# Four blocks of 32 columns in place of two of 64 for the last transform stage's products

## The chip, the cores and the metric

The kernel runs on one core of one Trainium2 chip. A core has a matrix engine (TensorE, PE in the profile; its loads of stationary operands are listed apart as PEld), a vector engine (VectorE, DVE), a scalar engine (ScalarE, ACT), GpSimd (POOL) and a queue engine (SyncE, SP) that issues transfers here. The metric is the device time of one execution in microseconds, as the median of several runs.

TensorE multiplies a stationary operand, which is loaded into an array of 128 rows by 128 columns, with a moving operand. A product may take only a part of the array: the rows are those of the contraction, the columns those of the output's partitions. The profile writes the part as rows*columns: 128*64 is a stationary operand of 128 rows in 64 columns.

## The reference

Two stages follow each other. The first is a long convolution in each of 128 channels, done with Fourier transforms; the second a feed-forward layer on its result.

```python
# x, v: (4, 12544, 128); pos_emb: (12544, 64)
h_filt = (np.maximum(pos_emb @ w1, 0.0) @ w2) * np.exp(-0.01 * pos)[:, None]
u = x * v
y = irfft(rfft(u, n=2 * S, axis=1) * rfft(h_filt, n=2 * S, axis=0), n=2 * S, axis=1)[:, :S]
attn = x * y
t = attn.reshape(4 * 12544, 128)
h = np.maximum(np.maximum(t @ moe_w1, t @ moe_w2), t @ moe_w3)   # 768 wide
out = h @ moe_w_out
```

All is 32-bit floating point.

## The kernel before

The transforms are products with tables. Positions are split in two: 12544 = 98 x 128. A forward transform has a first stage over the 98 (`u_products`), a twiddled second stage over the 128, the product with the filter's spectrum, and an inverse second stage; `g_quarter` does the second stages of two groups in one call, on blocks of 64 rows by 64 columns. Its results go to DRAM (`zd`), with 90 frequencies along one axis. The last transform stage is the inverse over these 90 frequencies. It is done tile by tile, where a tile is four of the 128 positions of a batch with all 98 of the other axis, 392 tokens, so there are 32 tiles in each of 4 batches, 128 in all.

For each tile these steps follow each other:

- `t_load` (line 705) brings `zt`, two halves of 90 x 512, and every second time `x`.
- `t_sums` (line 731) makes their sum and difference on VectorE or GpSimd.
- `t_last` (line 747) does the last stage's products on TensorE. For each of four positions `s` and two tables `a` it multiplies a stationary operand of 90 rows and 128 columns, taken from `zt`, with a table `f4p` of 49 moving columns. Each result goes to its own 49 columns of one PSUM bank. VectorE then multiplies the bank with `x` into `g`, the feed-forward layer's input.
- `up` and `down` (lines 766 and 777) do the feed-forward layer with 392 moving columns: for each of six blocks `f` two products of 128 rows and the maximum, and then a product into `ops`. In the last batch `products` (line 823) does the output products in another form.

Every one of these products goes through `halves_mm` (line 152) or is written in the same way by hand: one call becomes two, one on columns 0 to 63 and one on columns 64 to 127. The two write partitions 0 to 63 and 64 to 127 of the same bank:

```python
for h in range(2):
    nc.tensor.matmul(out[64 * h:64 * h + 64], lhsT[:, 64 * h:64 * h + 64], rhs,
                     start=start, stop=stop, skip_group_check=True)
```

The order of the work is fixed by the program's text, without a scheduler. While batch `b` goes through the feed-forward layer, the convolution of batch `b + 1` runs beside it: `conv_steps` (line 609) makes a list of its steps with a slot for each, six slots to a tile, and the main loop (line 1189) runs the steps of a slot behind that slot's `up` and `down`. `t_last` for the next tile is called in slot 2, 3 or 4 of the present one (`plan[i][2]`), so a tile's products are made some slots before its own `up` needs them. In the last batch (line 1266) there is no convolution beside it, and `t_last` is called twice for each pair of tiles. In the trace the products of `t_last` stand under line 156 with the outputs `cps`, `last` and, for the first tile, `hps`.

Of the kernel before, what the change touches and what calls it, by code (L numbers as in the profile page):

```python
# [91 lines left out]
def kernel(  # L92
# [15 lines left out]
    nc = tc.nc  # L108
    NG, _, _, B, NB = x.shape
    FO, S = posT.shape  # L110
    D = w2.shape[1]
# [40 lines left out]
    def halves_mm(out, lhsT, rhs, start, stop):  # L152
# [5 lines that stand above are left out]
# [543 lines left out]
    NT = P // 4  # L701
# [45 lines left out]
    def t_last(i, bank=None):  # L747
        zt = zts.pop(i)
        ps = bank or state["bank"]()
        own = i[0] == B - 1 and i[1] > 1  # L750
        g = (lp if own else hp).tile([D, 4, NB], FP32, tag="g", name="gt", bufs=4 if own else 3)
        y = ps[:, 0:N].rearrange("d (p n) -> d p n", p=4)

        h = NB // 2
        for s in range(4):
            for a in range(2):
                halves_mm(y[:, s, a * h:a * h + h], zt[a][:, s * D:(s + 1) * D],
                          f4p[:, i[0] > 0 and i[1] >= NT // 2, a, :], s == 0 and a == 0, True)
        y = y.rearrange("d p (a m) -> d p m a", a=2)
        xT = xTs.pop(i)  # L760
        nc.vector.tensor_tensor(out=g[:].rearrange("d p (m a) -> d p m a", a=2), in0=y,
                                in1=xT.rearrange("d p (m a) -> d p m a", a=2),
                                op=ALU.mult)
        gs[i] = g

    def up(i, f, tag="hid", bufs=3):
        rhs = gs[i][:].rearrange("d p n -> d (p n)")
        h = (hidp if tag == "hid" else lp).tile([P, N], FP32, tag=tag, name="hid", bufs=bufs)
        pa = next(hbanks)
        halves_mm(pa[:, 0:N], w_sb[1][:, f * P:(f + 1) * P], rhs, True, True)  # L770
        nc.scalar.activation(h[:], pa[:, 0:N], Relu)  # L771
        pb = next(hbanks)
        halves_mm(pb[:, 0:N], w_sb[2][:, f * P:(f + 1) * P], rhs, True, True)
        nc.vector.tensor_tensor(out=h[:], in0=h[:], in1=pb[:, 0:N], op=ALU.max)  # L774
        return h
# [386 lines left out]
    f4p = hp.tile([N1, 2, 2, NB // 2], FP32, name="f4p", bufs=1)  # L1162
# [26 lines left out]
    for n, (b, i) in enumerate(tiles[:LAST]):  # L1189
        if i == 0:  # L1190
            plan, pairs_from = plans[b]
        if n == 0:
            t_load(*tiles[0], (nc.sync, nc.gpsimd))
            t_load(*tiles[1])
            second_ = []
            for h, tag in enumerate(("eo", "cb")):
                top, both = u_products(2, 2 * h, 2, next(hbanks), tag)
                top()
                second_.append(both)
            spare = state["bank"]()  # L1200
            third = u_products(3)
            fourth = u_products(4, 0, 2, spare, "xs")
            t_sums(tiles[0], nc.vector)
            for fn in second_:
                fn()
            fourth[0]()
            t_last(tiles[0], next(hbanks))
            rest = u_products(4, 2, 2, ops.tile([D, 512], FP32, tag="ops", name="ps1"), "cb")
            rest[0]()
            fourth[1]()  # L1210
        for f in range(NF):

            if i < NT - 2:
                if f == 0:
                    t_load(*tiles[n + 2])
            elif i == NT - 1 and f < 2 and n + 1 + f < len(tiles):
                t_load(*tiles[n + 1 + f])
            turn_ = i == NT - 1
            if f == 4 and n + 1 == LAST:
                t_sums(tiles[n + 2], nc.vector)  # L1220
            h = up((b, i), f)
            if n == f == 0:
                rest[1]()
            if n == 0 and f in (1, 2):
                third((f - 1,))
            for a in range(2):
                if f == plan[i][a]:
                    t_sums(tiles[n + 1],
                           nc.vector if turn_ or i * NF > pairs_from else nc.gpsimd, (a,))
            late.append(((b, i), f, h))  # L1230
            if len(late) > 2:
                down(*late.pop(0))
            if f == plan[i][2]:
                t_last(tiles[n + 1])
            if f == 5 and n + 1 == LAST:
                t_last(tiles[n + 2])
            run(besides.pop(n * NF + f, ()))
# [28 lines left out]
    for i in range(0, NT, 2):  # L1266
        h = {}
# [69 lines left out]
```

## Time and profile before

| | |
|---|---|
| median of 3 runs | 2269.55 us (2269.53 to 2269.72) |
| span of the profiled execution | 2267.5 us |
| the median lies above that span by | 2.05 us |
| PE busy | 2252.4 us, 99% |
| PEld busy | 1356.9 us, 60% |
| DVE, ACT, POOL busy | 69%, 52%, 39% |
| granted TensorE clock | 1.00 of full speed between 300 us and the end |
| DMA share, 300 to 1850 us / 1850 to 2267 us | 0.90 / 0.22 |

The span is that of one profiled execution; its rows are sums and means over that execution. The time around it (start and end of the program) is not profiled; the difference to the median is taken for it. A row of the profile's groups gives the line, the engine, the operation, what is written and read, the part of the array, the shape of the moving operand, the number of records, and then busy time, mean duration of one in ns and idle time before it. In the timeline a row is a run of like instructions: start in us, duration in us, and the number of records. A matmul's duration reaches from its start to its modelled end, and successive matmuls overlap, so the pace is read from the starts and not from the durations.

The first 284 us are the prologue (filter, first batch's transform). From about 300 to 1847 us the feed-forward layer of three batches runs with the next batch's convolution beside it; the rest is the last batch alone.

### The profile page before, as it was taken

To read this page: it belongs to the slowest core of one execution; us is meant where nothing else is said; L and a number is where in the kernel's file an instruction comes from. 1 tells how busy PE (TensorE), PEld (TensorE's weight loads), DVE (VectorE), ACT (ScalarE), POOL (GpSimd) and SP (SyncE) were. 2 spreads that over 40 slices of the span, in tenths; PEclk is the share of its full clock that TensorE was granted. 3 is DMA by queue.
4 is the path that set the end of the run, shared out by engine and by line. 5 is a ranking of instruction groups with operands and counts; after the bars stand their busy time and mean duration, and the time that the engine had idled before them with its cause. 6 is when DMAs were issued, how large, how long until landed. Compare 5 with 4: busy or idle time off the path is not lost.

```text
span 2267.5 us, 68405 instructions
## 1 busy us (share of the span) xinstructions
PE 2252.4 (99%) x27855; PEld 1356.9 (60%) x27855; DVE 1563.7 (69%) x2859; ACT 1176.0 (52%) x2131; POOL 876.7 (39%) x1090
## 2 busy tenths in 40 slices
PE   9999999999999999999999999999999999999998
PEld 8999866555555556655555556655555556666665
DVE  5589967678778667668888757667888754454443
ACT  3688844466666534456666534456666522222222
POOL 1145434223333234323333234323333326666666
PEclk9999999999999999999999999999999999999999
DMA  8788999889989599989999699889999732222221
GB/s 194 179 248 277 298 201 183 168 201 233 243 220 248 158 187 185 174 190 239 241 236 238 181 180 185 160 195 239 232 245 232 194 82 56 58 70 67 56 56 23
DMA packets 473324, 411.03 MB, mean 181 GB/s; under 512 B 327997, under 2 KB 374526, under 8 KB 473009
## 3 DMA queue, kind: packets, MB, share of 16 engines
q1 hardware_dynamic: 445929, 329.31, 64.4%
q0 software_dynamic: 26288, 75.62, 10.9%
q8 instruction: 219, 3.59, 0.7%
q10 hardware_dynamic: 792, 1.72, 0.3%
q14 instruction: 96, 0.79, 0.1%
HBM read 262.84 MB, written 84.67 MB: 153 GB/s over the span
## 4 chain that ended last, share of the span: by engine, by line
PE 99%; DMA 0%; issue 0%; ACT 0%; POOL 0%; DVE 0%; POOLq 0%; ACTq 0%; DVEq 0%
PE hps L156 45%; PE ops L156 20%; PE ops L834 6%; PE cps L428 5%; PE ps L156 4%; PE cps L156 4%; PE cps L496 3%; PE ps L165 3%; PE cps L506 3%; PE sps L1066 2%; PE gps L1048 2%; PE last L156 1%; PE ps L380 1%; PE ps L342 1%; DMA wt<-wt_const 0%; DMA zt<-zd 0%
## 5 line engine op out<-in xcount | busy, mean ns | idle before, releaser
L156 PE MATMUL hps<-gt,w_sb 128*64 128x392 f32 x6144 | 1146.2, 494 | 0.1
L771 ACT ACTIVATE hid<-hps 128x392 f32<-128x392 f32 x768 | 384.1, 500 | 699.6 <-PE hps L156 680.6
L156 PEld LDWEIGHTS hps<-gt,w_sb 128*64 128x64 f32 x6144 | 421.2, 137 | 430.8 <-issue 401.3
L774 DVE TENSOR_TENSOR hid<-hid,hps 128x392 f32<-128x392 f32 x768 | 428.0, 557 | 335.6 <-PE hps L156 323.0
L156 PE MATMUL ops<-hid,wo_sb 128*64 128x392 f32 x2304 | 477.1, 492 | 0.0
L548 POOL TENSOR_TENSOR cb<-cb,xs 128x512 f32<-128x512 f32 x135 | 173.9, 1288 | 474.7 <-DVE xs L545 384.1
L156 PEld LDWEIGHTS ops<-hid,wo_sb 128*64 128x64 f32 x2304 | 166.0, 137 | 213.1 <-issue 213.1
L521 DVE TENSOR_TENSOR cb<-cps,eo 128x512 f32<-128x512 f32 (+1 forms) x288 | 175.1, 649 | 76.1 <-ACT eo L518 76.1
L445 DVE TENSOR_TENSOR spec<-cps,high 128x360 f32<-128x360 f32 (+1 forms) x186 | 139.2, 789 | 104.7 <-ACT high L440 104.7
L789 POOL DMA_DIRECT2D out_dram<-ot x96 | 75.6, 788 | 335.2 <-ACT ot L787 282.3
L536 ACT ACTIVATE xs<-cb 32x512 f32<-32x512 f32 x270 | 169.6, 628 | 21.1 <-DVE cb L521 12.1
L537 ACT COPY xs<-cb 32x512 f32<-32x512 f32 x270 | 166.3, 616 | 3.2
L440 ACT COPY high<-cps 128x360 f32<-128x360 f32 x93 | 73.9, 797 | 169.7 <-PE cps L428 144.9
L552 DVE TENSOR_TENSOR xs<-cb 128x256 f32<-128x256 f32 x270 | 144.4, 580 | 7.7 <-POOL cb L548 7.7
L428 PEld LDWEIGHTS cps<-f1q,uT 98*64 98x64 f32 x2960 | 125.4, 137 | 26.2 <-issue 24.3
L428 PE MATMUL cps<-f1q,uT 98*64 98x90 f32 x2960 | 130.9, 241 | 0.0
L396 POOL COPY planes<-ut 128x784 uint16<-128x784 uint16 x90 | 76.3, 847 | 119.8 <-DVE ut L375 114.1
L529 POOL DMA_DIRECT2D zd<-cb x135 | 92.4, 685 | 63.7 <-DVE cb L521 60.7
L156 PEld LDWEIGHTS cps<-f4p,even 90*64 90x64 f32 x1552 | 87.5, 138 | 35.9 <-issue 34.6
L858 POOL DMA_DIRECT2D out_dram<-o x128 | 77.5, 610 | 51.5 <-DVE o L851 49.1
L156 PE MATMUL cps<-f4p,zt 90*64 90x49 f32 x1552 | 95.8, 222 | 0.0
L156 PE MATMUL cps<-f4p,even 90*64 90x49 f32 x1552 | 94.5, 220 | 0.0
(152 smaller groups left out, 3150.5 us busy)
## 6 DMA issues: line engine op xcount, KB each, us to landing
ht<-hd SPq DMA_DIRECT2D x264, 256.0 KB, 6.5
wt<-wq_const SPq DMA_DIRECT2D x144, 256.0 KB, 6.2
zd<-cb POOLq DMA_DIRECT2D x135, 256.0 KB, 5.7
zt<-zd SPq DMA_DIRECT2D x384, 90.0 KB, 3.0
sq<-spec SPq DMA_DIRECT2D x264, 128.0 KB, 6.4
ut<-in_xr_dram SPq DMA_DIRECT2D x128, 196.0 KB, 4.0
ut<-in_vr_dram SPq DMA_DIRECT2D x128, 196.0 KB, 4.4
xT<-in_x_dram SPq DMA_DIRECT2D x256, 98.0 KB, 3.4
```

Of the source, the lines that this page charges most:

```text
L156: nc.tensor.matmul(out[64 * h:64 * h + 64], lhsT[:, 64 * h:64 * h + 64], rhs, start=start, stop=stop, skip_group_check=True)
L428: nc.tensor.matmul(ps[64 * c:64 * c + 64, 256 * i + h * N1:256 * i + (h + 1) * N1], t[:, 2 * ((at + i) % 8) + h].rearrange("n r t -> n (r ...
L445: nc.vector.tensor_tensor(out=spec[:, :, a, at:at + n], in0=v[:, 1], in1=highs[0], op=op)
L521: nc.vector.tensor_tensor(out=cb[:, a, lo:hi], in0=ps[:, lo:hi], in1=eo[:, lo:hi], op=op)
L529: nc.gpsimd.dma_start(zd[b][2 * z:2 * z + 2].rearrange("k c t a f -> (k c t) a f"), zss.pop(z))
L536: nc.scalar.mul(xs[at:at + 32], xt[at + 32:at + 64], -1.0)
L537: nc.scalar.copy(xs[at + 32:at + 64], xt[at:at + 32])
L548: nc.gpsimd.tensor_tensor(out=xts[g], in0=xts[g], in1=xs[:], op=ALU.add)
L552: nc.vector.tensor_tensor(out=ab[:, q], in0=y[:, 0], in1=y[:, 1], op=(ALU.subtract, ALU.add)[q])
L771: nc.scalar.activation(h[:], pa[:, 0:N], Relu)
L774: nc.vector.tensor_tensor(out=h[:], in0=h[:], in1=pb[:, 0:N], op=ALU.max)
L834: nc.tensor.matmul(ps[64 * c:64 * c + 64, 0:H2], w, rhs[:, H2 * c:H2 * c + H2], start=start, stop=True, skip_group_check=True)
```

## The change

The inner call of `t_last` on two halves of the columns is replaced by four calls on 32 columns each. Each writes 32 partitions of the same bank. The operands, the moving table, the order over positions and tables, and the sums in PSUM are the same; only `start`'s place in the call differs, since it is set for each of the four blocks at the first position and table as it was for each of the two.

```diff
         for s in range(4):
             for a in range(2):
-                halves_mm(y[:, s, a * h:a * h + h], zt[a][:, s * D:(s + 1) * D],
-                          f4p[:, i[0] > 0 and i[1] >= NT // 2, a, :], s == 0 and a == 0, True)
+                for q in range(4):
+                    nc.tensor.matmul(y[32 * q:32 * q + 32, s, a * h:a * h + h],
+                                     zt[a][:, s * D + 32 * q:s * D + 32 * q + 32],
+                                     f4p[:, i[0] > 0 and i[1] >= NT // 2, a, :],
+                                     start=s == 0 and a == 0, stop=True, skip_group_check=True)
```

Nothing else of the kernel changes.

## The prediction

> **What bounds the kernel now.** I read the page's busy shares first, then the chain, then the timeline of TensorE around one `t_last`, and last the timeline around other work that already uses the array in another division.
>
> ```profile
> PE   2252.4 (99%) x27855; PEld 1356.9 (60%) x27855; DVE 1563.7 (69%) x2859; ACT 1176.0 (52%) x2131; POOL 876.7 (39%) x1090
> ...
> PE 99%; DMA 0%; issue 0%; ACT 0%; POOL 0%; DVE 0%; POOLq 0%; ACTq 0%; DVEq 0%
> ...
> L156 PE MATMUL cps<-f4p,zt 90*64 90x49 f32 x1552 | 95.8, 222 | 0.0
> L156 PE MATMUL cps<-f4p,even 90*64 90x49 f32 x1552 | 94.5, 220 | 0.0
> ```
>
> TensorE is busy for 99% of the span, it is 99% of the chain that ended last, and the two rows of the changed products had no idle time before them. No other engine and no DMA sets the pace here, so whatever a `t_last` gains or loses on TensorE reaches the end one for one. The question is only how long one `t_last` holds the array. Each call appears as two records: 2 x 1552 here, 2 x 480 in the last batch and 32 at the start are 4096 records for 128 tiles x 16 calls.
>
> The timeline of one `t_last` (start, us, engine, line, operation, records):
>
> ```profile
> 995.87 0.27 PE L156 MATMUL cps<-f4p,even 90*64 90x49 f32 x4
> 995.97 0.29 PE L156 MATMUL cps<-f4p,zt 90*64 90x49 f32 x4
> ...
> 996.67 0.29 PE L156 MATMUL cps<-f4p,zt 90*64 90x49 f32 x4
> 996.79 1.50 PE L156 MATMUL hps<-gt,w_sb 128*64 128x392 f32 x8
> 998.12 0.83 PE L156 MATMUL ops<-hid,wo_sb 128*64 128x392 f32 x4
> 998.78 1.49 PE L156 MATMUL hps<-gt,w_sb 128*64 128x392 f32 x8
> ```
>
> From 995.87 to 996.79 it holds the array 0.92 us. The steps of four records are 0.117 us apart in the middle (995.97 to 996.67 are six steps), so a pair of records, one on each half of the columns, takes 58.4 ns. The `hps` group behind it takes 1.33 us to its successor where four pairs of 329 ns make 1.315, so the cost is 0.935 us, 16 pairs of 58.4 ns.
>
> The timeline around one `g_quarter` (64 rows by 64 columns, four blocks at once), entered from products on 128 rows by 64 columns and left to them again. The second fence is a narrower window on its entry:
>
> ```profile
> 1000.75 1.49 PE L156 MATMUL hps<-gt,w_sb 128*64 128x392 f32 x8
> 1002.07 0.83 PE L156 MATMUL ops<-hid,wo_sb 128*64 128x392 f32 x4
> 1002.83 0.67 PE L496 MATMUL cps<-sq,wt 64*64 64x128 f32 x16
> 1003.32 0.62 PE L506 MATMUL cps<-xs,wt 64*64 64x128 f32 x16
> 1003.75 0.62 PE L496 MATMUL cps<-sq,wt 64*64 64x128 f32 x16
> 1004.19 0.62 PE L506 MATMUL cps<-xs,wt 64*64 64x128 f32 x16
> 1004.74 1.54 PE L156 MATMUL hps<-gt,w_sb 128*64 128x392 f32 x8
> 1006.10 0.50 PE L156 MATMUL ops<-hid,wo_sb 128*64 128x392 f32 x2
> ```
> ```profile
> 1002.83 0.34 PE L496 MATMUL cps<-sq,wt 64*64 64x128 f32 x4
> ```
>
> The reader is to see two things. Four blocks do run at once: four records of 0.32 us or less began within 0.02 us, and sixteen take 0.435 us (1003.32 to 1004.19 is 0.87 for 32), 109 ns for a group of four. And the division costs something at its edges: 1002.07 to 1006.10 is 4.03 us, of which 2 pairs (0.657), 16 groups (1.745) and 4 pairs (1.315) explain 3.72. The other 0.31 us stand at the borders: 0.10 before the first record (the last pair's 329 ns from 1002.40 end at 1002.73), 0.05 more in the first group (0.49 to the next line in place of 0.435), 0.11 before `hps`, 0.05 in its first group.
>
> **The change, part by part.**
>
> *Instructions.* Each `t_last` issues 32 calls in place of 16, so 64 matmul and 64 load records in place of 32 and 32: 4096 more of each over the run. Order, operands, accumulation and all other engines' work are unchanged; VectorE's multiply still waits for the last call. No DMA or wait is added or moved.
>
> *How long a group takes.* A group becomes four blocks of 32 columns. What a matmul of 49 moving columns needs on its block follows from two rows: 329 ns at 392 columns and 109 at 128 give 0.833 ns a column, so 109 - 79 x 0.833 = 43 ns at 49. That is below the 58.4 seen today, so today's pair is held by something else, and the nearest row says by what: the weight load.
>
> ```profile
> 18.36 0.44 PEld L327 LDWEIGHTS ps<-back,winT 128*105 128x105 f32 x4
> 18.36 0.58 PE L327 MATMUL ps<-back,winT 128*105 128x64 f32 x4
> ```
>
> Four loads of 105 columns took 0.44 us in all, and one lasts 0.17, so they follow at (0.44 - 0.17) / 3 = 90 ns, while 64 moving columns would need 56. With 58.4 at 64 columns, a load costs (90 - 58.4) / 41 = 0.77 ns a column, and 32 columns come to 58.4 - 25 = 34 ns. So the load falls below the matmul, and a group is held by its 43 ns. This asks that loads of four column blocks overlap as those of two do today. I take 43; the bounds are 58.4 (loads share one path by columns, nothing gained) and, far above, 104 (four records at 26 ns, below). Stream: 16 x 43.3 = 693 ns in place of 935, a gain of 242 ns for each tile.
>
> *The borders.* Today's `t_last` has the division of its neighbours (all columns in halves, 90 and 128 rows), and I see no gap there. Blocks of 32 columns are a new division, entered and left 128 times; neighbours are always `up`, `down` or `u_products`, all in halves. Is it the rows or the columns that cost? The prologue has a change of columns alone:
>
> ```profile
> 61.81 1.72 PE L165 MATMUL ps<-f1q,uT 98*64 98x90 f32 x40
> 63.46 1.08 PE L380 MATMUL ps<-eye,ut 128*98 128x128 f32 x8
> 64.47 2.24 PE L165 MATMUL ps<-f1q,uT 98*64 98x90 f32 x52
> ```
>
> Twenty pairs of 77 ns (0.833 x 90 + 2.5) from 61.81 end at 63.36, and the transposes start at 63.46: 0.10. Eight of them at 109 ns are 0.87, but `f1q` starts 1.01 after: 0.14. So a change of columns costs 0.24 before the slower first group behind it, 0.29 with it. I take 0.31, the row with four blocks; the bounds are 0 (a change within column blocks is free) and 0.32.
>
> The Trainium skill, page "TensorEngine Tiling (Array Packing)", section "Key Properties", says that a change of tiling mode drains the array; it gives no price, and this trace does: about 0.1 us at each border. The same page's "Theoretical Speedup" table promises up to 4x for 32 columns; by that rule alone a `t_last` would fall from 0.935 to 0.47 us and the kernel to about 2210 us. The rows speak for the drain and for 43 ns a group.
>
> *Sum.* 693 + 310 = 1003 ns against 935: 68 ns more for each tile, x 128 = 8.7 us. The span goes from 2267.5 to 2276.2; the runs' median of 2269.55 lies 2.05 above the span, so 2278.3 us. I hold no cover against it: TensorE has no idle time at these places to swallow it, and what runs beside it only gets more slack.
>
> **The rivals.**
>
> 1. *No drain between column blocks* (faster). If halves and quarters count as one division, only the stream's gain is left: 242 x 128 = 31 us, 2238.6 us. For it: both leave the rows whole. Against: the prologue's change of columns alone costs 0.24. It decides below 0.24 us for the two borders.
> 2. *Loads or issue hold the group.* If loads of the four blocks share their path, a group stays at 58.4 and the borders are pure loss: 310 x 128 = 40 us, 2309. For it: four loads with the same rows appear nowhere here. Against: two halves' loads overlap today, or a pair would need twice one load. An intermediate 50 ns gives +22 us.
> 3. *No four at once, or a floor for each record.* The tightest row of small products, 64 moving columns on four blocks, goes at 30 ns a record and less (line below; 26 in blocks of 64 records). At 26 ns, 64 records take 1664 ns: (1664 + 310 - 935) x 128 = 133 us, 2403. With two blocks at a time: 16 x 87 + 310 - 935, 98 us, 2368. For it: that row. Against: its loads last 197 ns where others last 133, so they may be the brake, and `g_quarter`'s four records began within 0.02 us.
>
> ```profile
> 20.63 3.02 PE ps L342 x100
> ```
>
> The page "TensorE: Matmul & The Clock Gate", section "Wait — 56ns, not 53.3ns?", puts a floor of about 25 ns between the starts of small matmuls. By that rule the sum would be near rival 3's; the starts within 0.02 us of four blocks speak against it across blocks.
>
> **How the numbers follow.** The main case (drain of 0.29 to 0.32, groups of 43 to 47 ns) has 0.62 and gives +48 to +137 ns a tile, 2275.7 to 2287 us; its centre is the forecast, 2278.3. Rival 2 in all its degrees has 0.13 (2287 to 2310), rival 3 has 0.07. Rival 1 in full has 0.08, and borders of half the price or so 0.10 (from 2253 to 2274), of which about half falls within 0.2% of before. A 0.2% change is 4.5 us, about what a measurement of this kernel can tell from none. So faster 0.13, same 0.06, slower 0.81. The range from 2268 to 2310 takes in the main case, rival 2 and the upper part of the cheap borders; outside are rivals 1 and 3.
>
> **What would show it.** In the profile after, the rows read 90*32 with 6208, 1920 and 64 records; between `t_last`'s first record and `hps` about 0.78 to 0.80 us (15 groups of 43, the last stream, then the gap of 0.1), 0.1 us of gap before the first record, and `hps` and its like behind it with a slower first group. Groups of 58 ns would show rival 2, records 20 ns or more apart rival 3, no gap rival 1. It would be wrong if TensorE waited anywhere for what comes out of `t_last`, or if the division were changed at a different price for 32-column blocks than for 64 and 98.

## The result and the profile after

The changed kernel takes 2284.02 us (2282.83 to 2288.86 in four runs) against 2269.64 before: a ratio of 1.0066, 95% interval 1.0052 to 1.0081. It is 14.4 us slower. Its four runs spread over 6 us where the four before spread over 0.4; but in the comparisons below, 13 and 21 runs of the kernel before spread over 4 and 5 us, so this spread is no sign of the change. The forecast was 2278.3 (8.7 us slower), the range 2268 to 2310. The profiled execution has a span of 2282.8 us and a time of 2284.58; the span before was 2267.5, so 15.3 us are to be found.

The page of the changed kernel, its lines on busy shares, the instruction queue, the chain and the new loads; the last line is that of the same loads before:

```profile
PE 2262.9 (99%) x31951; PEld 1328.0 (58%) x31951; DVE 1564.3 (69%) x2859; ACT 1176.1 (52%) x2131; POOL 877.0 (38%) x1090
...
q8 instruction: 251, 4.11, 0.8%
...
PE 98%; DMA 1%; issue 0%; SPq 0%; DVE 0%; POOL 0%; ACT 0%; POOLq 0%; ACTq 0%; DVEq 0%
...
L758 PEld LDWEIGHTS cps<-f4p,even 90*32 90x32 f32 x3104 | 65.0, 108 | 59.3 <-issue 49.5
...
L156 PEld LDWEIGHTS cps<-f4p,even 90*64 90x64 f32 x1552 | 87.5, 138 | 35.9 <-issue 34.6 <-DVE zt L740 0.6 <-DVE xs L545 0.4
```

TensorE issues 4096 more records of each kind, as said, and a load lasts 108 ns where it lasted 138. It is busy for only 10.5 us more, though; 4.8 us of the 15.3 are time in which it is idle (span less busy, 15.1 us before and 19.9 after). The queue of instructions brings 251 packets in place of 219.

The timeline of two `t_last` in the changed kernel:

```profile
1852.57 1.49 PE L156 MATMUL hps<-gt,w_sb 128*64 128x392 f32 x8
1853.89 0.83 PE L156 MATMUL ops<-hid,wo_sb 128*64 128x392 f32 x4
1854.65 0.29 PE L758 MATMUL cps<-f4p,even 90*32 90x49 f32 x8
1854.76 0.27 PE L758 MATMUL cps<-f4p,zt 90*32 90x49 f32 x8
...
1855.28 0.27 PE L758 MATMUL cps<-f4p,zt 90*32 90x49 f32 x8
1855.48 1.54 PE L156 MATMUL hps<-gt,w_sb 128*64 128x392 f32 x8
1856.85 0.83 PE L156 MATMUL ops<-hid,wo_sb 128*64 128x392 f32 x4
1857.61 0.29 PE L758 MATMUL cps<-f4p,even 90*32 90x49 f32 x8
```

Eight records, two groups of four blocks, follow at 0.087 us (1854.76 to 1855.28 is six steps): 43.7 ns a group. All four blocks work at once. The borders are there too: the last `ops` pair from 1854.22 would end at 1854.55, the first record stands at 1854.65; 1855.28 plus 0.087 is 1855.37 and `hps` starts at 1855.48; and `hps` needs 1.37 to its successor in place of 1.315.

Laid tile against tile, the two traces drift apart by 54 to 55 ns with nearly every `t_last`, from the first batch to the last: 128 x 0.0545 = 7.0 us. Some 8.0 us of the rest come in eight single steps, all in the first three batches, the largest of 4.2 us at the 81st tile; at five of the eight TensorE is idle for 0.34 to 2.09 us, which the profile puts to "issue". One more step, of 1.0 us, belongs to neither part: at 312 us TensorE waited 0.87 us for VectorE (`hid`), at a place which the changed kernel reached 0.6 us earlier than the kernel before. 7.0 + 8.0 + 1.0 - 0.6 is 15.4, the 15.3 but for rounding. At the 81st tile the trace shows this:

```profile
1580.57 0.29 PE L758 MATMUL cps<-f4p,even 90*32 90x49 f32 x8
...
1581.40 1.54 PE L156 MATMUL hps<-gt,w_sb 128*64 128x392 f32 x8
1582.77 0.83 PE L156 MATMUL ops<-hid,wo_sb 128*64 128x392 f32 x4
1583.53 0.67 PE L496 MATMUL cps<-sq,wt 64*64 64x128 f32 x16
1584.02 0.62 PE L506 MATMUL cps<-xs,wt 64*64 64x128 f32 x16
1584.45 0.62 PE L496 MATMUL cps<-sq,wt 64*64 64x128 f32 x16
1584.89 0.60 PE L506 MATMUL cps<-xs,wt 64*64 64x128 f32 x12
1587.58 0.44 PE L506 MATMUL cps<-xs,wt 64*64 64x128 f32 x4 [2.09 <-issue]
1587.94 2.87 PE L156 MATMUL hps<-gt,w_sb 128*64 128x392 f32 x8
1590.60 1.23 PE L156 MATMUL ops<-hid,wo_sb 128*64 128x392 f32 x4
```

TensorE stops in the middle of a run of like products that wait for nothing; the profile can only say "issue". Counted in the trace, a packet of the instruction queue started at 1585.12 and landed at 1586.25, and the products went on 1.33 us after that. Some 272 records, loads and matmuls, stand within the 4.9 us ahead of the gap, 128 of them in `t_last` and 120 in `g_quarter`. Then `hps` takes 2.66 us to its successor in place of 1.33. The table by windows shows why (window, its length, busy times, granted clock, DMA share, GB/s):

```profile
1585.00:1589.00 4.00, 1.91 (x24) 0.98 (x18) 1.03 (x2) 0.00 (x0) 1.25 (x1) 0.87 0.87 299
1589.00:1592.00 3.00, 3.00 (x14) 1.11 (x12) 1.07 (x2) 0.97 (x2) 0.00 (x0) 0.60 1.04 199
1592.00:1595.00 3.00, 3.00 (x22) 1.33 (x20) 1.30 (x4) 2.40 (x5) 0.68 (x1) 1.00 1.07 216
```

The granted clock falls behind the gap: 0.13 x 4 + 0.40 x 3 = 1.7 us of it are lost, 3.4 us at half speed, so a gap of 2.1 us costs about 4.

### The profile page after: what moved, and what is told of

It is laid out like the page before. It is cut to its first block, busy times and chain, and to the rows that moved or that the text cites. A ratio compares the mean times of both kernels' runs of the same rounds, so it can differ in the third digit from the quotient of the medians.

```text
span 2282.8 us, 76597 instructions
## 1 busy us (share of the span) xinstructions
PE 2262.9 (99%) x31951; PEld 1328.0 (58%) x31951; DVE 1564.3 (69%) x2859; ACT 1176.1 (52%) x2131; POOL 877.0 (38%) x1090
## 3 DMA queue, kind: packets, MB, share of 16 engines
q8 instruction: 251, 4.11, 0.8%
## 4 chain that ended last, share of the span: by engine, by line
PE 98%; DMA 1%; issue 0%; SPq 0%; DVE 0%; POOL 0%; ACT 0%; POOLq 0%; ACTq 0%; DVEq 0%
PE hps L156 45%; PE ops L156 19%; PE ops L837 6%; PE cps L428 5%; PE ps L156 4%; PE cps L758 4%; PE cps L496 3%; PE ps L165 3%; PE cps L506 3%; PE sps L1069 2%; PE gps L1051 2%; PE last L758 1%; PE ps L380 1%; PE ps L342 1%; DMA ut<-in_vr_dram 0%
## 5 line engine op out<-in xcount | busy, mean ns | idle before, releaser
L758 PEld LDWEIGHTS cps<-f4p,even 90*32 90x32 f32 x3104 | 65.0, 108 | 59.3 <-issue 49.5
L540 DVE TENSOR_TENSOR cb<-cb,ht 128x512 f32<-128x512 f32 x135 | 92.3, 683 | 2.5 <-ACT xs L537 2.0
L375 DVE TENSOR_TENSOR ut<-ut 128x392 f32<-128x392 f32 x128 | 78.5, 615 | 20.4 <-DMA ut<-in_vr_dram 18.9
```

The source lines that it names most:

```text
L758: nc.tensor.matmul(y[32 * q:32 * q + 32, s, a * h:a * h + h], zt[a][:, s * D + 32 * q:s * D + 32 * q + 32], f4p[:, i[0] > 0 and i[1] >= NT ...
```

## The experiments

My theory had two parts now: +54 ns a tile, from groups and borders as predicted, and gaps where TensorE runs out of instructions, because a `t_last` has twice as many and a packet comes late while transfers are dense. The rival was one cost spread over all tiles, 14.4 / 128 = 112 ns each; a second rival for the gaps was something else that comes late at those places.

### The change in the last batch alone

```diff
-                halves_mm(...)
+                if i[0] == B - 1:
+                    ...  # four blocks of 32
+                else:
+                    halves_mm(...)
```

> Four blocks of 32 columns only in the last batch's 32 tiles; the other 96 tiles keep two of 64. Theory (two parts): each tile costs +54 ns on TensorE (groups of 43.7 ns, 0.29 us at the borders), and beside it TensorE ran out of instructions in a few places while transfers are dense. The last batch has a DMA share of 0.22, so here only the first part: 32 x 0.054 = +1.7 us, 2271.3, no gaps in which TensorE waits for issue, and hardly any spread between runs. Rival (the whole +14.4 us is one cost spread over the tiles, 112 ns each): +3.6 us, 2273.2.

2271.87 us against 2270.05 (ratio 1.0007, interval 0.9997 to 1.0016): +1.8. The interval reaches from -0.7 to +3.6 us, so the times alone don't tell the theory from its rival or from no change; the trace does. In it a pair of tiles of the last batch takes 26.07 us in place of 25.96, 55 ns a tile, and no gap for issue stands in the last batch. That is the first part alone. The spread was not small, as I had expected, but 3.8 us, like that of the kernel before.

### The change in the first three batches alone

The same edit with `i[0] < B - 1`.

> Four blocks of 32 columns only in the first three batches' 96 tiles. Theory: 96 x 0.054 = 5.2 us, plus all of the gaps for issue, 7 to 8 us in the profiled run: +11 to +14 us, 2281 to 2284, with a spread of microseconds between runs. Rival of one spread cost: +10.8 us, 2280.4, without gaps.

2284.2 us, ratio 1.006 (1.0045 to 1.0075): +14.1 with 96 tiles, which is nearly all of the loss. The interval, +10 to +17 us, does not exclude the 10.8 of a spread cost; the trace does. A tile costs 54 ns there too, and the gaps are there, at the same instructions: ahead of matmul records 10395, 10776 and 23375 of the trace, exactly where the changed kernel has three of its five idle gaps. The other two, of 0.34 and 0.65 us, did not come again beyond 0.15 us, so a gap does not come in every execution. The spread cost is out.

### Instructions shifted by half a packet

```diff
     warm_up(3)
+    ps = next(turns_)
+    for _ in range(16):
+        halves_mm(ps[:, 0:8], warm[:, 0:P], warm[:, 0:8], True, True)
+    next(turns_)
```

> The changed kernel with 16 idle calls of 8 moving columns more in the prologue: 32 products on each half's worth, 64 matmul and 64 load records, which shifts all later TensorE instructions by half a packet of 256 and costs under 1 us of its own. Theory of supply (a gap comes where a dense stretch meets the end of a packet): the gaps of the changed kernel before records of L506, L496 and hps near 613, 641, 1149, 1585 and 1798 us vanish and others appear elsewhere; the time may differ by several us to either side, 2277 to 2292. Rival (a gap belongs to a place in the work, such as a transfer or a sum that comes late there): the gaps stay at the same steps, 2284 to 2285.

2291.56 us, ratio 1.0092 (1.0078 to 1.0107). The gaps left their places in the work and others opened. Who TensorE waited for (total, times, longest):

```profile
PE hps L156 <- issue: 3.9, 2, 2.4
```

The largest is behind 1070 us now; others of the trace are at 488, 1219 and 1580 us, with smaller steps of 0.2 to 0.5 us at 633 and 1285 us, and at the places of the changed kernel's gaps near 613, 641, 1149 and 1798 us there are none beyond 0.2 us. The one at 1580, 0.39 us long, is 191 matmul records of the same work ahead of the changed kernel's largest, in another `g_quarter`. So a gap belongs to the place of a packet's end in a dense stretch, not to a step of the work. The run is 7.5 us above the changed kernel by the medians, and 4.7 by the two profiled executions. Of these 4.7 some 3.7 lie ahead of 340 us, in the prologue and a stretch at half clock at 303 us; behind that the moved gaps cost 1.0 us more than those of the changed kernel.

### Fewer transfers, and the same without the change

```diff
     def w_load(x):
-        w = wp.tile([P, 2, 2, 2, 64], FP32, tag="w", name="wt")
-        nc.sync.dma_start(...)
+        if "w" not in kept:
+            w = kept["w"] = wp.tile([P, 2, 2, 2, 64], FP32, tag="w", name="wt")
+            nc.sync.dma_start(...)
+        w = kept["w"]
```

and likewise in `h_load`.

> The changed kernel with the filter's spectrum and the quarter twiddles brought once in place of for every group (h_load and w_load), so later groups are multiplied with the first group's values; the instructions of TensorE are the same. If a packet of instructions is late because transfers are dense, the gaps for issue shrink or vanish: 2277 to 2280, +7 to +10 us of per-tile cost being all that is left. If the request itself comes late whatever the transfers do (rival), the gaps stay: 2283 to 2285.

> The kernel before with the same transfers left out, as the measure of the run with fewer transfers. TensorE has no gap there, so no change: 2269.5 within 1 us.

The changed kernel takes 2279.3 us (1.0038, 1.0024 to 1.0051), the kernel before 2270.3 (1.0000, 0.9991 to 1.0009). The middle stage with fewer transfers, and the same stage of the changed kernel (columns as above):

```profile
300.00:1850.00 1550.00, 1548.22 (x20736) 813.66 (x20736) 1134.76 (x2009) 852.05 (x1538) 507.82 (x603) 1.00 0.59 135
```
```profile
300.00:1850.00 1550.00, 1545.09 (x20567) 815.68 (x20564) 1128.52 (x1997) 850.71 (x1534) 509.15 (x603) 1.00 0.89 204
```

With a DMA share of 0.59 in place of 0.89, and as many instructions, no gap for issue is left after 320 us, and the traces part by 54 ns a tile from the third tile to the last, 6.6 us in all. The gaps need both: the dense instructions and the busy transfers. The profiled execution is 9.9 us longer than the one before, and about 3 of these lie ahead of the third tile: this execution had a stretch at half clock in its prologue, which accounts for 1.7, and at 315 us the same wait for VectorE as the changed kernel has at 312, here 0.97 us.

### Products of two tiles together, in the last batch

```diff
-            if j in (5, 8) and i + 2 < NT:
-                t_last((b, i + 2 + (j > 5)))
+            if j == 8 and i + 2 < NT:
+                t_last((b, i + 2))
+                t_last((b, i + 3))
```

with four blocks of 32 for tiles 2 to 31 of the last batch and two of 64 for all others.

> Two of 64 columns everywhere but in the last batch's tiles 2 to 31, where four blocks of 32 are used and the products of two tiles stand one behind the other, so that two borders serve two tiles. Theory of groups and borders: 15 pairs x (2 x (0.699 - 0.935) + 0.29) = -2.7 us, 2266.9, and no gap for issue since transfers are light there. If borders cost nothing (rival): 30 x -0.236 = -7.1 us. If the per-tile cost has nothing to do with borders (rival): 30 x 0.054 = +1.6 us.

2267.91 us against 2270.71, ratio 0.9988 (0.9979 to 0.9998): 2.8 us faster than before where 2.7 was worked out, and the interval leaves out both rivals. One such pair of tiles:

```profile
1887.85 0.29 PE L759 MATMUL last<-f4p,even 90*32 90x49 f32 x8
...
1889.19 0.27 PE L759 MATMUL last<-f4p,zt 90*32 90x49 f32 x8
1889.39 1.54 PE L156 MATMUL hps<-gt,w_sb 128*64 128x392 f32 x8
...
1913.63 0.29 PE L759 MATMUL last<-f4p,even 90*32 90x49 f32 x8
```

The second tile's records follow the first's at the pace of 43.7 ns a group, without a border. A pair takes 25.78 us (1887.85 to 1913.63) where it took 25.96 before: 2 x (0.699 - 0.935) + 0.29 = -0.18. The order itself has no part in this: in the run with pairs of 64 columns (below) a pair of the last batch takes 25.96 us as well. So the border's price is shown by halving its number, and it is what turns the faster groups into a loss.

### Products of two tiles together, everywhere

In the first three batches I moved the sums and the products so that tiles 2 and 3, 4 and 5 and so on have theirs together.

```diff
-            if f == plan[i][2]:
+            if f == plan[i][2] and (i == 0 or i % 2):
                 t_last(tiles[n + 1])
+                if 0 < i < NT - 1:
+                    t_last(tiles[n + 2])
```

Loads and sums of the second tile go with it. In this first form the second tile's products can take a bank that `g_fold` has not read yet, so a part of the convolution is not the reference's in either of the next two; their instructions are the same in number.

> Four blocks of 32 columns, and the products of two tiles made one behind the other wherever the text allows, so that the array is divided anew 68 times in place of 128. Theory: streams gain 128 x (0.935 - 0.699) = 30.2 us, borders cost 68 x 0.29 = 19.7 us, net -10.5 us, 2259, if the instructions keep up; 256 of them then stand within 1.4 us, so gaps for issue may give back 5 to 20 us. Rival of one spread cost of 112 ns a tile that has nothing to do with borders: +14 us, 2284.

> The order of work of the run before (products of two tiles together) with two blocks of 64 columns as before the change. Theory: no border, no gap, 2269.6 within 1 us; it shows that the order itself costs or brings nothing. Rival (the order matters by itself, by sums or loads that come late): several us slower, with TensorE waiting for VectorE or a transfer before these products.

2325.17 us with 32 columns (1.0235, 1.0219 to 1.0251), 2299.77 with 64 (1.0123, 1.0106 to 1.0140). I missed both: the order itself costs 30 us, and the smaller blocks another 25 in place of bringing 10.5. With 32 columns the trace has twelve gaps for issue behind 300 us, 22.5 us in all; with 64 it has none. The costliest row of them:

```profile
PE hps L156 <- issue: 14.6, 5, 4.6
```

From the first product of the last batch to the start of the last one, where transfers are light, 32 columns are 2.8 us faster than 64 (398.71 against 401.48), as the sum says; all of the loss is in the three batches with dense transfers.

The second form runs the two tiles' products behind the other steps of their slot, when the bank has been read; the earlier call is left for a batch's first and last tile alone:

```diff
             run(besides.pop(n * NF + f, ()))
+            if f == plan[i][2] and i % 2 and i < NT - 1:
+                t_last(tiles[n + 1])
+                t_last(tiles[n + 2])
```

> As the run with pairs of 32, but in the first three batches the two tiles' products come behind the other steps of their slot, when the bank that the second one takes has been folded. Theory: streams and borders give -10.5 us against 2269.7; what lies above 2259 is waiting, for issue (256 instructions within 1.7 us) and for the sums and banks of the new order, which the same order with 64 columns shows apart. With the waits of the earlier pair of runs: 2285 to 2325.

> The same order with two blocks of 64 columns: no border and few instructions, so it shows what the order costs by itself: 2270 to 2300 us. The difference to the run with 32 columns is -10.5 us if instructions keep up, and above nothing if they don't.

2377.49 us (1.0474, 1.0455 to 1.0492) and 2357.89 (1.0385, 1.0370 to 1.0401): both above what I expected, and 19.6 us apart the wrong way. Who TensorE waited for with 32 columns:

```profile
PE cps L758 <- DVE spec L445: 21.0, 11, 3.0
PE cps L758 <- DVE cb L521: 20.8, 17, 1.9
PE cps L506 <- DVE xs L552: 9.0, 17, 0.8
PE hps L156 <- issue: 6.5, 3, 2.9
```

Products of two tiles in one slot need both banks, and those wait for VectorE's folds and sums. With 64 columns the same two waits come to 18.8 and 19.4 us, so this order is worse for a reason of its own, and it does not answer what pairing could bring in these batches. An order with banks enough for it was not tried.

## Why the prediction was right, and what it lacked

- **What bounds.** Right for the products themselves: the chain after is 98% TensorE's again, and the cost of a tile reached the end one for one (54 to 55 ns a tile from the third tile to the last). It left out that TensorE can also stand still for its own instructions.
- **The group.** 43 ns forecast from two rows, 43.7 measured. That four blocks' loads overlap held too: narrowing the blocks to 32 brought the pace to the matmul's own. That the old pair was held by its loads fits this and is the likeliest reason, but no run changed the loads alone. Rivals 2 and 3 are out.
- **The borders.** 0.31 us taken, 0.29 found (935 + 54.5 - 16 x 43.7). The gaps are those of the `g_quarter` row, about 0.1 on each side; the first group is 0.02 us slower than the others, where 0.05 was read there, and from the first record to `hps` it is 0.83 us in place of the 0.78 to 0.80 forecast. Rival 1 is out: a change of column blocks alone has its price at both borders. The rule on drains of the page "TensorEngine Tiling (Array Packing)" of the Trainium skill held, and the runs price it.
- **The sum for a tile.** 68 ns forecast, 54.5 measured: 7.0 us in place of 8.7.
- **The step that failed.** "No DMA or wait is added or moved", and with it that nothing else could cost: the 8192 more instructions are themselves brought by transfers, 32 packets more. In this kernel's middle stage a packet can come too late, and the gaps and the half-speed clock behind the longest made 8.0 us, more than half of the loss. The forecast had the sign and the mechanism of one half; that the range held the result was luck as to the other half. The main case reaches up to 2287 us because it allowed groups of 47 ns, and the range to 2310 because it allowed for rival 2; neither was found. "Issue" was named in rival 2, but as a limit on the pace of a group, which it is not.

## What to carry to other kernels

Blocks of fewer columns made products of few moving columns faster here, from 58 to 44 ns for the same work, most likely because the weight load held them; but each change of the division costs about 0.29 us in and out together, so they pay only in stretches that gain more than that: one tile's 0.24 us of gain is too little, two tiles' 0.47 was enough in the last batch. In the three batches with dense transfers no order that was tried made it pay. Count the instructions of such an edit as transfers: look for stretches in which several hundred stand within a few microseconds while DMA is busy, and for gaps that the profile calls "issue" in the middle of like work.

## What the runs showed of the hardware

TensorE's instructions come in packets: 219 of them were 3.59 MB and 251 are 4.11 MB, 16.4 KB each. 32 more packets for 8192 more records make 256 instructions a packet. The gaps ended 1.2 to 1.5 us behind the landing of a packet, so I take 1.3 us after it landed as the time when a packet could be used. Behind 300 us TensorE had by then started, sequencer's records counted, at most 410 records beyond 256 times the packet's number in the run before; in the changed run it was 449 to 452 in the seven latest cases, which are seven of the eight steps, and with the shifted instructions 449 in the eight latest. With fewer transfers it was at most 395. So 449 is where it stands still. The densest 256 records of the middle stage took 7.8 us before the change and 4.3 after it. A late packet starts late rather than travels long: a packet took 1.1 us at the median with either share of transfers, but at its start TensorE stood up to 447 records beyond that mark with a DMA share of 0.89, and up to 321 with 0.59. The Trainium skill, page "Runtime: NRT & Kernel Launch", section "Instruction fetch mechanics", has the blocks of 256 instructions, which agrees, and calls the cost of crossing one mostly hidden; it was hidden before the change and with a DMA share of 0.59, and not with 0.89 and twice the instructions in `t_last`.

A gap of 2.1 us was followed by 3.4 us at half clock, and so were those of 2.2 us (first three batches alone) and 2.4 us (shifted instructions). The page "TensorE: Matmul & The Clock Gate", section "What's actually happening", has the half rate and a window of 3.4 us, which agrees with the stretch; that a stretch can follow a gap shorter than the window is what these traces add. What sets it is not shown: a gap of 1.4 us at 488 us of the shifted run had none behind it, and in the run of the last batch alone one began at 300.2 us behind waits of 0.84 and 0.40 us.
